# Moving small route steps to VectorE and the decode subtractions of attention to GpSimd

## The chip, the cores and the metric

The kernel runs on one core of a Trainium2 chip. The metric is the device time of one execution, in microseconds; the median of three runs is compared. The engines are named as in the profile: PE is TensorE's matmul side and PEld its weight loads, DVE is VectorE, ACT is ScalarE, POOL is GpSimd, SP is SyncE, which here only issues DMAs. Each engine runs its own instructions strictly in the order in which they were written.

## The reference

Three layers follow each other: local attention with a distance bias, a mixture of experts with one expert per token, and a mixing layer (two Fourier transforms and a wide two-matmul block). Only the first two matter here.

```python
# attention, per batch b and head h (B=2, H=8, S=768, D=64; 8 global keys, 96 local keys)
scores = q @ k.T / sqrt(D) - slope[h] * dist     # kept where key is global or local
a = exp(scores - max); a = a / (sum(a) + 1e-9)
x = a @ v                                        # heads side by side: (B, S, 512)

# routing, token by token: the expert may be the previous token's
fresh = argmax(x @ w_gate)
e = fresh if s == 0 or sigmoid(x @ w_local) < 0.5 else previous e
p = softmax(x @ w_gate)
out = p[e] * (relu(x @ w1[e]) @ w2[e])           # E=8 experts, 512 -> 1024 -> 512
```

## The kernel before

**Attention** (`fast_attention`). The 768 positions are cut into six tiles `i` = 0 to 5 of 128. A unit `n` is one tile, one batch entry `b` and one half `g` of the heads (four heads), so there are 24 units, four for each tile. The loop over `n` is a software pipeline written out by hand. In round `n` it writes, among others:

- `out(n - 2, 1)`: ACT copies the second half of a transposed probability tile out of PSUM (line 166);
- `keep(n - 3)`: DVE copies the product with v out of PSUM (line 179);
- `scores(n)`: PE (line 132), `rowmin(n)`: four DVE instructions that add the bias and find the row extreme `nm` (line 141);
- `transp(n - 1, 0)` and `transp(n - 1, 1)`: PE transposes (line 160), `expo(n)`: four exponentials on ACT (line 150) that also sum into `den`, and then the addition of 1e-9 to `den` (line 151);
- `upright(n - 3)`: PE (line 184), `norm(n - 3)`: DVE divides by `den` (lines 196, 199, 201);
- `values(n - 2)`: PE (line 174).

`patch_k` (line 104) and `patch_v` (line 109) put the eight global keys and values into the head of a tile that the next tile will read as its neighbour.

**Routing** (`Route.run`). After the fourth unit of a tile, a generator starts that finds the experts of its tokens. It is advanced between the steps of the later rounds, so a tile's route steps lie in the rounds of the next tile. It makes `lg` (line 481), the largest logits (507, 510), `gn` and `gf` (508, 514), `pe` (513), two PE transposes of `gn` and `gf` (517, 518), `rows` on ACT (521), the sum `su` (524, 528, 535), two scans over the tokens (532 `ex`, 541 `cu`), two small PE matmuls (546, 547), the rank `rk` (555), the probabilities into `xrow` (557) and the place `pos` of each token (565). Then SP writes the rows to `xs` (568) and POOL writes the token list by an indirect DMA (569). The engine `X` takes the steps 508, 513, 528 and 557: GpSimd, and VectorE for the last tile.

After tile 3 (`i == NT - 3` with NT = 6) SP reads the head of the list back (line 580) and POOL gathers the first tokens of expert 0 by an indirect DMA into `st.x0` (line 583), which `early` uses for expert 0's first matmuls.

**Decoding of expert pieces.** Four expert weight pieces are loaded during attention and split into a rounded high half and the rest: ACT casts (line 1007) and DVE subtracts (line 1009), in columns of 512. The table `TAKES` sets the rounds: group 0, 1, 2 and 3 with four columns each, 16 pairs in all. `Ring.take` uses DVE unless it is given another engine by `eng`.

**Behind attention** the list is read, tokens are gathered and the experts run (PE at work nearly throughout), then the mixing layer.

Of the kernel before, what the change touches and what calls it, by code (L numbers as in the profile page):

```python
# [18 lines left out]
ALU = mybir.AluOpType  # L19
# [8 lines left out]
NT = S // P  # L28
# [24 lines left out]
def load_kq(nc, st, io, i, pairs=((0, B * H // 2),)):  # L53

    if i >= NT:
        return
    for h, n in pairs:
        nc.sync.dma_start(st.kq[i][:, :, h:h + n], io["kq"][i, :, :, h:h + n])


def fast_attention(tc, st, io, route):
    nc = tc.nc
    V, A, G, T = nc.vector, nc.scalar, nc.gpsimd, nc.tensor
    KS = 3
    HP = B * H // 2
    with ExitStack() as ctx:
# [12 lines left out]
        four, last = views(st.raws, PIECES), views(more, NT - PIECES)  # L79
# [7 lines left out]
        def load_v(i):  # L87
            nc.sync.dma_start(vs[:, i % KS], io["v"][i])
# [45 lines left out]
        def rowmin(n):  # L134
            u = live[n]
            u.nm = wk.tile([P, 4], F32, name="nm")
            u.t = wk.tile([P, 4, 256], F32, name="t", bufs=3)
            for k in range(2):
                for j in range(2):
                    x = 2 * k + j  # L140
                    V.tensor_tensor_reduce(  # L141
                        out=u.t[:, x, :u.W], in0=u.sp[:, j, k, :u.W], in1=bias[:, 4 * u.g + x, u.b0:u.b0 + u.W],
                        scale=-0.125, scalar=3.0e38, op0=ALU.add, op1=ALU.min,
                        accum_out=u.nm[:, x:x + 1])

        def expo(n):
            u = live[n]
            u.den = wk.tile([P, 4, 1], F32, name="den", bufs=4)
            for x in range(4):
                A.activation(u.t[:, x, :u.W], u.t[:, x, :u.W], AF.Exp, bias=u.nm[:, x:x + 1], scale=-1.0, accum_out=u.den[:, x])  # L150
            G.tensor_scalar(u.den, u.den, 1e-9, None, op0=ALU.add)

        def transp(n, k):
            u = live[n]
# [7 lines left out]
        def out(n, k):  # L162
            u = live[n]
            if k == 0:
                u.p = wk.tile([P, 4, 2, P], F32, name="p")
            A.copy(u.p[:, 2 * k:2 * k + 2, :u.nk], u.tp[k][:, :, :u.nk])  # L166
# [9 lines left out]
        def keep(n):  # L176
            u = live[n]
            u.o = wk.tile([P, 2, P], F32, name="o")
            V.tensor_copy(u.o, turned)
# [44 lines left out]
        def far():  # L224
            d = local(prev, 0)
            V.tensor_tensor(d, d, gl, op=ALU.max)
            load_v(1)
            yield
            yield from tables(0, 256)
            load_kq(nc, st, io, 2)  # L230
            load_kq(nc, st, io, 3)
# [10 lines left out]
        bg = Background()  # L242
        bg.add(near)
        units = [(i, b, g) for i in range(NT) for b in range(B) for g in range(2)]
# [12 lines left out]
        def step(k):  # L257

            for at, g, lo, hi in TAKES:
                if k == at:  # L260
                    bg.add(st.ring.take("e", g, cols=512, follow=False, part=(lo / 4, hi / 4)))
            route.slot = k % 4
            bg.step()
            for _ in range(AHEAD.get(k, 0)):
                next(ahead, None)

        for n in range(N + 3):
            if ok(n):
                i, b, g = units[n]
                first = (b, g) == (0, 0)  # L270
                if (b, g) == (1, 0) and 0 < i < NT - 1:
                    load_v(i + 1)
                if first and i > 0:
                    load_kq(nc, st, io, i + 3)
                if i >= 2 and (b, g) == ((1, 0) if i < NT - 1 else (0, 0)):

                    st.ring.load(i - 2)
            if n == 1:
                bg.add(far())
            k = 4 * (n - N)  # L280
            if ok(n - 2):
                out(n - 2, 1)
            if ok(n - 3):
                keep(n - 3)
            if ok(n):
                scores(n)
                rowmin(n)
                if units[n][2]:
                    patch_k(*units[n][:2])
            if ok(n - 3) and not ok(n - 1):  # L290
                upright(n - 3)
                norm(n - 3)
            step(k)
            if n < len(BUSY):
                keep_busy(nc, st, ps_t.tile([P, 2, 2, P], F32, name="tp").rearrange("p a b n -> p (a b n)"), BUSY[n])
            if ok(n - 1):
                transp(n - 1, 0)
            if ok(n):
                expo(n)
            if ok(n - 1):  # L300
                out(n - 1, 0)
            step(k + 1)
            if ok(n - 1):
                transp(n - 1, 1)
                if ok(n - 3):
                    upright(n - 3)
                    norm(n - 3)
            step(k + 2)
            if ok(n - 2):
                values(n - 2)  # L310
                if units[n - 2][2]:
                    patch_v(*units[n - 2][:2])
            step(k + 3)
            if n == 2:
                G.tensor_copy(gk, st.kq[0][:, 0, :, :GMAX])
            if ok(n - 3):
                live.pop(n - 3)
# [10 lines left out]
def general_attention(tc, st, io, route):  # L328
# [3 lines left out]
    with ExitStack() as ctx:  # L332
# [18 lines left out]
        for i in range(NT):  # L351
# [11 lines left out]
            for b in range(B):  # L363
                x = rt.tile([P, ROW], F32, name="xrow")
                xs.append(x)
                for h in range(H):
# [16 lines left out]
                    V.tensor_tensor(t, t, far, op=ALU.add)  # L383
                    V.tensor_reduce(out=m, in_=t, op=ALU.max, axis=AX.X)
                    V.tensor_scalar(m, m, -1.0, None, op0=ALU.mult)
                    A.activation(t, t, AF.Exp, bias=m)
                    V.tensor_reduce(out=m, in_=t, op=ALU.add, axis=AX.X)
                    V.tensor_scalar(m, m, 1e-9, None, op0=ALU.add)
# [40 lines left out]
class Route:  # L429
# [31 lines left out]
    def run(self, i, xs, parts=None):  # L461
        nc, st, sb = self.tc.nc, self.st, self.sb
        V, A, G, T = nc.vector, nc.scalar, nc.gpsimd, nc.tensor
# [9 lines left out]
        pp = sm[:, 0:B]  # L473
        other = sm[:16, 4:5]
        last, soon = i == NT - 1, i in (NT - 3, NT - 2)
        X = V if last else G
        to = lambda s, n=1: self.at(None if last else s, n)
        from2, from1 = st.pairs[:16, 0:16], st.pairs[:16, 16:32]
        lg = sb.tile([P, B, NL], F32, name="lg")
        if parts is not None:  # L480
            V.tensor_reduce(out=lg.unsqueeze(3), in_=parts.rearrange("p b h e -> p b e h"), op=ALU.add, axis=AX.X)
        else:
# [23 lines left out]
        for b in range(B):  # L506
            V.max(m8[:, b], l8[:, b])
        X.tensor_scalar(gn, z.to_broadcast([P, B, E]), GATE, None, op0=ALU.is_ge)
        for b in range(B):
            V.max_index(ix[:, b], m8[:, b], l8[:, b])  # L510
        yield from to(3 if soon else 1)
        V.tensor_copy(fr, ix[:, :, :1])
        X.tensor_tensor(pe, l8, m8[:, :, :1].to_broadcast([P, B, E]), op=ALU.subtract)
        V.scalar_tensor_tensor(gf, z.to_broadcast([P, B, E]), GATE, fr.to_broadcast([P, B, E]),
                               op0=ALU.is_lt, op1=ALU.mult)
# [7 lines left out]
        yield from to(1)  # L523
        V.tensor_reduce(out=su, in_=pe, op=ALU.add, axis=AX.X)
        if last:
# [3 lines left out]
        if last:  # L529
# [3 lines left out]
                             op0=ALU.mult, op1=ALU.add)  # L533
# [8 lines left out]
                             op0=ALU.mult, op1=ALU.add)  # L542
# [1282 lines left out]
```

## Time and profile before

| | |
|---|---|
| median of three runs | 658.94 us (657.78 to 660.36) |
| the profiled execution | 660.04 us |
| its span in the trace | 658.3 us |
| granted TensorE clock, mean | 0.983 |
| busy: PE / PEld / DVE / ACT / POOL | 95% / 77% / 60% / 42% / 13% |

The span is the time from the first to the last instruction of the trace; the 1.7 us beside it are around the program. The chain of waits that the profile follows back from the end begins only at about 308 us, so it says nothing of attention, which takes the first 115 us; attention is read from the timelines of the engines. In a timeline a row gives the start, the duration, the engine, the line and the operation, and in brackets the idle time ahead of it with what ended it. Starts of neighbouring rows can lie closer than a duration, since instructions of one engine overlap at their ends.

### The profile page before, as it was taken

To read this page: it belongs to the slowest core of one execution; us is meant where nothing else is said; L and a number is where in the kernel's file an instruction comes from. 1 tells how busy PE (TensorE), PEld (TensorE's weight loads), DVE (VectorE), ACT (ScalarE), POOL (GpSimd) and SP (SyncE) were. 2 spreads that over 40 slices of the span, in tenths; PEclk is the share of its full clock that TensorE was granted. 3 is DMA by queue.
4 is the path that set the end of the run, shared out by engine and by line. 5 is a ranking of instruction groups with operands and counts; after the bars stand their busy time and mean duration, and the time that the engine had idled before them with its cause. 6 is when DMAs were issued, how large, how long until landed. Compare 5 with 4: busy or idle time off the path is not lost.

```text
span 658.3 us, 9969 instructions
## 1 busy us (share of the span) xinstructions
PE 622.8 (95%) x3621; PEld 509.3 (77%) x3622; DVE 392.3 (60%) x906; ACT 279.3 (42%) x562; POOL 83.0 (13%) x133
## 2 busy tenths in 40 slices
PE   7999985869999999999999899999999999999997
PEld 3777754659988998897867687877788888888886
DVE  4789885418958688844368977899451141254112
ACT  5888783218455666654433533542221121141110
POOL 1133222230431332320100000000000000000000
PEclk9999997869999999999999999999999999999999
DMA  8354460557898798884053133453010010100001
GB/s 295 150 195 135 131 99 20 133 167 259 327 367 297 255 319 296 311 335 142 10 206 140 65 127 129 134 185 129 0 65 0 1 65 1 65 0 1 0 1 64
DMA packets 25219, 92.49 MB, mean 140 GB/s; under 512 B 7660, under 2 KB 8812, under 8 KB 17216
## 3 DMA queue, kind: packets, MB, share of 16 engines
q1 hardware_dynamic: 19408, 77.44, 34.7%
q0 software_dynamic: 4736, 10.56, 4.4%
q10 hardware_dynamic: 1008, 3.65, 1.5%
q8 instruction: 35, 0.57, 0.4%
q14 instruction: 32, 0.26, 0.2%
HBM read 81.03 MB, written 14.84 MB: 146 GB/s over the span
## 4 chain that ended last, share of the span: by engine, by line
PE 39%; DVE 11%; ACT 2%; issue 1%; DMA 1%; DVEq 0%; ACTq 0%
PE h L1637 17%; PE acc L1653 5%; PE acc L1652 5%; PE acc L1651 5%; DVE dec L1033 1%; DVE dec L1035 1%; PE y L1142 1%; PE more L1192 1%; PE more L1142 1%; PE h L1192 1%; DVE dec L1031 1%; DVE dec L1029 1%; DMA u<-x 1%; PE f L1603 1%; DVE wide L987 1%
## 5 line engine op out<-in xcount | busy, mean ns | idle before, releaser
L1642 DVE SCALAR_TENSOR_TENSOR hl<-h,hh 128x512 fp32r<-128x512 f32 x48 | 33.0, 688 | 118.0 <-ACT hh L1641 118.0
L1641 ACT ACTIVATE hh<-h 128x512 fp32r<-128x512 f32 x48 | 28.6, 596 | 153.2 <-PE h L1637 153.2
L1009 DVE TENSOR_TENSOR wide<-raws,wide 128x1024 fp32r<-128x1024 f32 (+2 forms) x46 | 50.5, 1111 | 25.8 <-ACT wide L1007 25.7
L150 ACT ACTIVATE t<-t,nm 128x256 f32<-128x256 f32 (+1 forms) x96 | 45.8, 478 | 9.5 <-DVE nm L141 9.5
L1007 ACT CAST wide<-raws 128x1024 fp32r<-128x1024 f32 (+2 forms) x46 | 43.3, 957 | 5.3 <-PE acc L1653 3.4
L1637 PE MATMUL h<-un0h,wide 128*128 128x512 f32 (+1 forms) x136 | 42.5, 378 | 0.1
L1652 PE MATMUL acc<-wide,hh 128*128 128x512 f32 x96 | 37.8, 394 | 0.0
L1653 PE MATMUL acc<-wide,hl 128*128 128x512 f32 x96 | 37.6, 391 | 0.0
L1651 PE MATMUL acc<-wide,hh 128*128 128x512 f32 x96 | 37.5, 391 | 0.0
L141 DVE CUSTOM_DVE_ANT_0 t<-sp,bias 128x256 f32<-128x256 f32 (+1 forms) x96 | 32.7, 395 | 6.7 <-ACT p L166 2.9
L1165 ACT ACTIVATE hh<-h 128x512 fp32r<-128x512 f32 x28 | 16.7, 598 | 31.7 <-PE h L1162 29.4
L1072 POOL DMA_INDIRECT xg<-xs,ent x23 | 27.5, 1196 | 15.7 <-issue 6.1
L160 PE MATMUL tp<-consts,t 128*128 128x128 f32 x176 | 27.2, 290 | 2.4 <-ACT p L166 1.9
L1637 PEld LDWEIGHTS h<-un0h,wide 128*128 128x128 f32 x136 | 25.0, 188 | 5.0 <-ACT un0h L1413 0.3
L1162 PE MATMUL h<-xh,wide 128*128 128x256 f32 x192 | 28.4, 284 | 0.2
L160 PEld LDWEIGHTS tp<-consts,t 128*128 128x128 f32 x176 | 19.6, 144 | 11.0 <-ACT p L166 6.6
L1162 PEld LDWEIGHTS h<-xh,wide 128*128 128x128 f32 x192 | 25.5, 192 | 1.0 <-ACT sl5h L1007 0.5
L1166 DVE SCALAR_TENSOR_TENSOR hl<-h,hh 128x512 fp32r<-128x512 f32 x28 | 19.2, 685 | 11.8 <-ACT hh L1165 9.6
L1637 PE MATMUL h<-un0l,wide 128*128 128x512 f32 (+1 forms) x68 | 25.6, 377 | 0.0
L174 PE MATMUL sm<-p,vs 128*64 128x128 f32 x352 | 24.5, 279 | 0.0
L166 ACT COPY p<-tp 128x512 f32<-128x512 f32 (+1 forms) x48 | 24.2, 533 | 0.0
L1035 DVE SCALAR_TENSOR_TENSOR dec<-raws,dec 128x1024 int32<-128x1024 int32 x18 | 22.0, 1225 | 0.6
(450 smaller groups left out, 1635.5 us busy)
## 6 DMA issues: line engine op xcount, KB each, us to landing
raws<-we SPq DMA_DIRECT2D x30, 1024.0 KB
raws<-wm SPq DMA_DIRECT2D x17, 1024.0 KB
raws<-wmf SPq DMA_DIRECT2D x7, 1024.0 KB
wmf<-dec POOLq DMA_DIRECT2D x8, 512.0 KB, 9.0
xs<-xrow SPq DMA_DIRECT2D x12, 260.0 KB
vs<-v SPq DMA_DIRECT2D x6, 512.0 KB
raws<-kq SPq DMA_DIRECT2D x3, 1024.0 KB
u<-x SPq DMA_DIRECT2D x6, 512.0 KB
```

Of the source, the lines that this page charges most:

```text
L141: V.tensor_tensor_reduce(out=u.t[:, x, :u.W], in0=u.sp[:, j, k, :u.W], in1=bias[:, 4 * u.g + x, u.b0:u.b0 + u.W], scale=-0.125, scalar=3.0 ...
L150: A.activation(u.t[:, x, :u.W], u.t[:, x, :u.W], AF.Exp, bias=u.nm[:, x:x + 1], scale=-1.0, accum_out=u.den[:, x])
L160: T.transpose(u.tp[k][:, j, c], u.t[:, 2 * k + j, c * P:(c + 1) * P], st.ident)
L1007: (first or nc.scalar.copy)(hi[:, cs], raw[:, cs])
L1009: (eng() if callable(eng) else eng or nc.vector).tensor_tensor(lo[:, cs], raw[:, cs], hi[:, cs].bitcast(F32), op=ALU.subtract)
L1162: T.matmul(ps[:, u], w[:, f], x[:, k], start=n == 0, stop=n == 11)
L1637: nc.tensor.matmul(ps[:, c], a[:, k], x[:, k, c], start=n == 0, stop=n == 11)
L1641: nc.scalar.activation(hh, ps, AF.Relu)
L1642: nc.vector.scalar_tensor_tensor(hl, ps, 0.0, hh.bitcast(F32), op0=ALU.max, op1=ALU.subtract)
L1651: T.matmul(acc[c], hh[:, cs], h2, start=first, stop=False)
L1652: T.matmul(acc[c], hh[:, cs], l2, start=False, stop=False)
L1653: T.matmul(acc[c], hl[:, cs], h2, start=False, stop=last)
```

## The change

There are four edits, all within attention and its routing:

1. the addition to `den` (line 151) is made by VectorE for the units of the last tile, and by GpSimd for the others as before;
2. the subtraction of the decode pairs in attention (line 1009) is given to GpSimd;
3. `patch_k` and `patch_v` are left out for the last tile, which has no next tile;
4. `X` is VectorE for the last two tiles (4 and 5) and not for the last one alone.

```diff
-            G.tensor_scalar(u.den, u.den, 1e-9, None, op0=ALU.add)
+            (G if u.i < NT - 1 else V).tensor_scalar(u.den, u.den, 1e-9, None, op0=ALU.add)
...
             for at, g, lo, hi in TAKES:
                 if k == at:
-                    bg.add(st.ring.take("e", g, cols=512, follow=False, part=(lo / 4, hi / 4)))
+                    bg.add(st.ring.take("e", g, cols=512, follow=False, part=(lo / 4, hi / 4), eng=lambda: G))
...
                 scores(n)
                 rowmin(n)
-                if units[n][2]:
+                if units[n][2] and units[n][0] < NT - 1:
                     patch_k(*units[n][:2])
...
                 values(n - 2)
-                if units[n - 2][2]:
+                if units[n - 2][2] and units[n - 2][0] < NT - 1:
                     patch_v(*units[n - 2][:2])
...
         last, soon = i == NT - 1, i in (NT - 3, NT - 2)
-        X = V if last else G
+        X = V if i >= NT - 2 else G
```

The first place is on POOL at the end of attention. `list<-dest,pos` is the list write of a tile, `vs<-xs,ent_89` the gather of expert 0's first tokens, `gn`, `pe`, `su` and `xrow` are the route steps of tile 4, `wide` is a low half of an expert piece. Before:

```order
L569 DMA list<-dest,pos 12416x2 x2
L151 TENSOR_SCALAR den<-den 128x4
L583 DMA vs<-xs,ent_89 128x520
L508 TENSOR_SCALAR gn<-lg 128x16
L513 TENSOR_TENSOR pe<-lg,m_1489 128x16
L104 COPY kq<-gk 128x4x8
L151 TENSOR_SCALAR den<-den 128x4
L528 TENSOR_SCALAR su<-su 128x2
L557 TENSOR_SCALAR xrow<-pe,su 128x8 x2
L569 DMA list<-dest,pos 12416x2 x4
```

And after:

```order
L557 TENSOR_SCALAR xrow<-pe,su 128x8 x2
L1009 TENSOR_TENSOR wide<-raws,wide 128x512 x2
L569 DMA list<-dest,pos 12416x2 x2
L1009 TENSOR_TENSOR wide<-raws,wide 128x512 x2
L583 DMA vs<-xs,ent_89 128x520
L1009 TENSOR_TENSOR wide<-raws,wide 128x512 x4
L569 DMA list<-dest,pos 12416x2 x4
```

Behind the gather there stand now four subtractions and the list writes, and no route step of tile 4.

The second place is on DVE, the stretch in which tile 4's gates are made; `lg` are its logits, `o` is `keep`'s copy. Before:

```order
L1009 TENSOR_TENSOR wide<-raws,wide 128x512
L196 RECIPROCAL rs<-den 128x4
L199 TENSOR_TENSOR lgp<-mi,rs 128x40
L201 TENSOR_TENSOR xrow<-mi,rs 128x256
L481 TENSOR_REDUCE lg<-lgp 128x20
L507 MAX m_1489<-lg 128x8 x2
L510 MAX_INDEX ix<-m_1489,lg 128x8 x2
L512 CAST fr<-ix 128x2
L514 SCALAR_TENSOR_TENSOR gf<-lg,fr 128x16
L1009 TENSOR_TENSOR wide<-raws,wide 128x512
L179 COPY o<-sm 128x256
```

And after:

```order
L151 TENSOR_SCALAR den<-den 128x4
L196 RECIPROCAL rs<-den 128x4
L199 TENSOR_TENSOR lgp<-mi,rs 128x40
L201 TENSOR_TENSOR xrow<-mi,rs 128x256
L481 TENSOR_REDUCE lg<-lgp 128x20
L507 MAX m_1488<-lg 128x8 x2
L508 TENSOR_SCALAR gn<-lg 128x16
L510 MAX_INDEX ix<-m_1488,lg 128x8 x2
L512 CAST fr<-ix 128x2
L513 TENSOR_TENSOR pe<-lg,m_1488 128x16
L514 SCALAR_TENSOR_TENSOR gf<-lg,fr 128x16
L179 COPY o<-sm 128x256
```

Two subtractions are gone from there, `gn` and `pe` have come in, and at the head stands the addition to `den`, which reads what the exponentials of the same round sum up.

## Rows read from the trace of the kernel before

**Rows 1.** The page: busy time, share of the span and instructions of each engine.

```profile
PE 622.8 (95%) x3621; PEld 509.3 (77%) x3622; DVE 392.3 (60%) x906; ACT 279.3 (42%) x562; POOL 83.0 (13%) x133
```

**Rows 2.** Stretches: length, each engine's busy time (instructions), granted clock, DMA share, GB/s.

```profile
97.00:104.20 7.20, 0.26 (x3) 0.06 (x2) 3.56 (x19) 1.21 (x3) 1.62 (x4) 0.73 0.01 1
...
180.00:260.00 80.00, 79.36 (x503) 71.03 (x504) 62.40 (x79) 47.51 (x61) 21.10 (x21) 1.00 0.84 298
```

**Rows 3.** Timeline of POOL around 103 us: start, duration, operation, idle time and releaser.

```profile
102.67 1.11 POOL L583 DMA_INDIRECT vs<-xs,ent  x1 [5.54 <-DMA ent<-list]
103.81 0.28 POOL L508 TENSOR_SCALAR gn<-lg 128x16 bf16<-128x16 f32 x1
```

**Rows 4.** Timeline of SP's queue: the read of the list's head.

```profile
99.63 0.33 SPq L580 DMA_DIRECT2D ent<-list  x1
```

**Rows 5.** Timeline of PE in attention.

```profile
56.19 1.14 PE L132 MATMUL sp<-raws 64*128 64x256 f32 x8
...
58.21 0.66 PE L160 MATMUL tp<-consts,t 128*128 128x128 f32 x4 [0.29 <-ACT p L166]
...
60.64 1.13 PE L132 MATMUL sp<-raws 64*128 64x256 f32 x8
...
64.48 0.49 PE L132 MATMUL sp<-raws,kq 64*128 64x128 f32 x4
...
79.50 0.22 PE L517 MATMUL sm<-identb,gn 128*16 128x128 bf16 x1 [1.38 <-DVE o L179]
...
87.03 0.20 PE L546 MATMUL sm<-cu,consts 16*16 16x1 f32 x2
...
104.14 0.28 PE L517 MATMUL sm<-identb,gn 128*16 128x128 bf16 x1 [6.94 <-POOL gn L508]
```

**Rows 6.** Timeline of ACT: exponentials and their sums.

```profile
54.61 0.51 ACT L150 ACTIVATE t<-t,nm 128x256 f32<-128x256 f32 x1 [0.42 <-DVE nm L141]
...
87.51 0.19 ACT L150 ACTIVATION_READ_ACCUMULATOR t<-t,nm 128x1 f32 x1
...
94.67 0.51 ACT L150 ACTIVATE t<-t,nm 128x256 f32<-128x256 f32 x1 [0.43 <-DVE nm L141]
...
105.46 0.50 ACT L150 ACTIVATE t<-t,nm 128x256 f32<-128x256 f32 x1
```

**Rows 7.** Timeline of DVE in attention.

```profile
53.21 0.69 DVE L1009 TENSOR_TENSOR sl0l<-raws,sl0h 128x512 fp32r<-128x512 f32 x1
...
88.71 0.75 DVE L1009 TENSOR_TENSOR wide<-raws,wide 128x512 fp32r<-128x512 f32 x1 [0.75 <-ACT wide L1007]
...
96.19 0.17 DVE L196 RECIPROCAL rs<-den 128x4 f32<-128x4 f32 x1
...
98.17 0.18 DVE L514 SCALAR_TENSOR_TENSOR gf<-lg,fr 128x16 bf16<-128x16 f32 x1
...
108.25 0.17 DVE L535 RECIPROCAL su<-su 128x2 f32<-128x2 f32 x1 [0.37 <-POOL su L528]
...
109.50 0.46 DVE L541 TENSOR_TENSOR_SCAN cu<-consts,cu,oh 16x128 f32<-16x128 f32 x1
...
111.91 0.41 DVE L179 COPY o<-sm 128x256 f32<-128x256 f32 x1
```

**Rows 8.** Waits of ACT from 46 to 135 us: total, times, longest.

```profile
ACT t L150 <- DVE nm L141: 5.2, 9, 0.9
```

**Rows 9.** Timeline of POOL: a full-width copy, two small copies, the last list write.

```profile
6.56 0.64 POOL L454 COPY iw<-consts 128x512 f32<-128x512 f32 x1
...
69.78 0.51 POOL L104 COPY kq<-gk 128x32 f32<-128x32 f32 x1 [0.58 <-PE sp L132]
...
88.71 0.20 POOL L104 COPY kq<-gk 128x32 f32<-128x32 f32 x1
...
123.98 0.97 POOL L569 DMA_INDIRECT list<-dest,pos  x1 [6.80 <-DVE cnt L604]
```

**Rows 10.** Timeline of DVE behind attention: the two probability products on VectorE.

```profile
122.33 0.35 DVE L557 TENSOR_SCALAR xrow<-pe,su 128x8 f32<-128x8 f32 x2
```

## The prediction

> **What bounds the kernel now.** I read the page first, then a table of stretches, then the timelines of the four compute engines through attention, since the change touches nothing behind it. By the page PE is busy 95% of the span [rows 1], so the question is where PE is not busy within attention, and whether time won there reaches the end. In the experts it does: from 180 to 260 us PE works 79.36 of 80 us [rows 2], the weights are loaded as that work frees their buffers, and the first gathers wait for the token list that attention leaves. So I count a microsecond won in attention as a microsecond at the end.
>
> Within attention one hole stands out. From 97.0 to 104.2 us PE works 0.26 us of 7.2, and the granted clock of that stretch is 0.73, between the two levels of 1.2 and 2.4 GHz [rows 2]. The timelines say why. POOL stands at the gather of expert 0's first tokens, which waits for the list's head, issued on SP at 99.63; the gather starts at 102.67 after 5.54 us of idling, and only behind it comes `gn` of tile 4, at 103.81 [rows 3, 4]. PE's transposition of `gn` at 104.14 has waited 6.94 us for it [rows 5], and in PE's queue stand all the transposes of the last units. `gn` itself needs only the logits, which DVE has by 97.4. It is a wait in a queue, not for data.
>
> The rest of attention is nearer to its bounds. PE starts the scores of a unit at 60.64 and of the next at 64.48 [rows 5], 3.84 us with no wait. The unit ahead, 56.19 to 60.64, took 4.45: 0.13 of route matmuls more, and 0.48 lost where a transpose had to wait until 58.21 for ACT's copy. ACT was that late because it had itself stood 0.42 us at 54.61 for `nm` from DVE [rows 6], and DVE had just spent 0.69 on a subtraction at 53.21 [rows 7].
>
> **The change part by part.** All times are on the clock of the profiled execution.
>
> *The 16 subtractions leave DVE.* That is 16 of about 0.69 us [rows 7], 11 us of DVE time; but DVE is not the bound. ACT's waits for `nm` are 5.2 us in all [rows 8], which is the most ACT can win, and PE wins less, because it is at its own pace of 3.84 us whenever ACT is on time. Up to 80 us PE has three holes that hang on DVE: 0.48 in group 0, the same 0.47 in group 1, and the 1.38 at 79.50, where the transposition of tile 3's gates waits for `gf` and `keep`'s copy at the end of a DVE queue that has just made two subtractions [rows 5]. The lower bound of this part is 0.95 (the third hole stays), the upper 2.3 (all close). Without its two subtractions the DVE queue ahead of 79.50 is 1.2 us shorter, so I take **2.0**. Below nothing I see only by way of the port, a rival below.
>
> *On POOL* a subtraction of 128x512 does not occur in this trace. The nearest row is a copy of 128x512, 0.64 us [rows 9]; two inputs may double it, 1.28, and I take 1.2. Pairs come every 4.4 us in the decode rounds, so POOL, 13% busy [rows 1], holds them easily. The Trainium skill (GPSIMD Engine Reference, "Performance versus the Vector engine") calls GpSimd the wrong choice for ordinary elementwise work and gives 4497 ns for such an operation of 2048 columns; an estimate from that page is a quarter, 1.12 us, and the sum would be the same by it. Behind the subtractions stand the list writes. Those of tile 3 come after two subtractions whose casts are done by 89.7, so they are through by about 92, when `pos` is made; the gather and the reading of the list's head are not held. The last four run behind the gather, to about 109, and the list of tile 4 is only wanted at about 110.
>
> *Tile 4's route steps go to DVE.* This removes the wait of 6.94. What is late next is DVE's own chain, because the third addition to `den` of tile 5 now stands at its head and waits for the exponentials of its round: they start at 94.67 in the trace [rows 6], at 94.5 with DVE relieved, and four of 0.49 and the reading of the sum end at 96.55; `den` is done at 96.7. From `rs` at 96.19 to the end of `gf` at 98.35 [rows 7] is 2.16 us, plus `gn` and `pe`, 0.35 for both at the 0.18 of their neighbour: `gf` at 99.2, `keep`'s copy at 99.6, PE at **99.66 instead of 104.14: 4.5 us**. ACT's last exponentials then start at 101.0 instead of 105.46 [rows 6].
>
> Some of it is given back. The last `den` waits for these exponentials to 103.0, and ten DVE instructions now stand behind it which in the trace went ahead: `cu` comes at 105.4 instead of 109.50 [rows 7], 4.1 won. In the trace `su` had its own wait for POOL there, at 108.25, and it goes. Then two products of `xrow`, 0.35 by the same pair on VectorE at 122.33 [rows 10], stand ahead of `keep`'s copy at 111.91 [rows 7]: 3.8 won. From there on the queues are the same as before. So this part is **3.8**, at most 4.5 (nothing given back), at least 2.5 if PE's clock falls all the same in the 2 us in which it still stands still.
>
> *The additions to `den` on DVE* cost 0.15 each, but the wait counts: the first of them stands ahead of `cu` of tile 3, and PE's small matmul on `cu`, at 87.03 [rows 5], has all of PE's work behind it. The sums are read to 87.70 [rows 6], so it starts at about 88.45 and PE loses 1.4 us. Its cover is ACT: the next exponentials start at 90.17 in the trace, and with DVE's subtraction gone `nm` is there at 90.2 in spite of the wait. PE runs a unit behind ACT and takes the loss out of what it had ahead, so I cost it at nothing; without the cover it is 1.4.
>
> *The patches of the last tile* are two copies of 0.2 us on POOL and two small DMAs on SP. Nobody reads them; SP's rows of tile 4 no longer queue behind a patch, but are wanted much later. Nothing.
>
> Sum: 2.0 + 3.8 = 5.8 us. The profiled execution took 660.04, so 654.2 by its own time; it is 1.1 above the median of the runs, 658.94, and the changed kernel's median comes to **653.1**.
>
> **The rivals.**
>
> *The two engines get in each other's way.* A POOL copy of 128x32 takes 0.20 at 88.71 but 0.51 at 69.78 [rows 9], where a DVE subtraction was under way; at 88.71 both started together, and there DVE's took 0.75 instead of 0.69 [rows 7]. So the one that comes second waits. Now POOL's are the long ones, and DVE's scan `cu` and rank `rk`, each with two inputs, could wait for them: `rk` of tile 3, some 0.85, and behind the gather, where four subtractions follow each other without a gap, `cu` and `rk` of tile 4, 0.6 and 1.2. That is 2.7 of the 5.8: 655.8. For it: the row at 69.78. Against it: most of DVE's work here reads one input from PSUM, and other POOL rows beside such work are not lengthened. The Trainium skill (SBUF — State Buffer, "Who interferes with whom") has this as a rule, an exclusive lock for an operation of DVE with two SBUF inputs against a GpSimd one that reads SBUF, held by whichever starts first; by it this rival would be the forecast. The rows at 69.78 and 88.71 agree with it; how often the two meet, no row tells.
>
> *The additions to `den` cost what I put at nothing*, and the holes before 80 us stay at half: 5.8 less 1.4, less 1.0, less a further 1.0 for the tail: 656.5. For it: DVE now waits for ACT four times while ACT waits for DVE in each round, a ring with little slack. Against it: the working above, unit by unit.
>
> *Better than forecast:* nothing is given back in the tail, and the full 2.3 before it with a further 1 of the 5.2 us of ACT's waits: 651.1.
>
> *Slower: POOL becomes the bound.* Four subtractions and the list write of tile 4 stand between the gather, done at 104.3, and the last tile's list write, wanted at 120.2 (123.98 [rows 9] less 3.8); the list takes 2.7. That is room for four of 3.3 us. From 4.75 us each the whole gain is gone, and at 6 us each the time is 663.9. For it: the operation has no row here. Against it: the copy of the same width at 0.64.
>
> *The change doesn't do what it says* would be that PE's transposition finds another wait on POOL; but tile 4 then has nothing on POOL ahead of its list write, so this has no chance of its own.
>
> **How the numbers follow.** Forecast 0.53, at 651.9 to 654.5; the port 0.20; `den` 0.12; better 0.09; slower 0.06. The range runs from 650.2, a microsecond under the better case for what a median of three moves, to 657.4, a microsecond over the worst of the cases that gain; outside are the slower case and the ends. Half a per cent, 3.3 us, is about what a measurement of this kernel can tell from no change, so faster means below 655.6: the forecast, the better case and a third of the port case, 0.69. Within: the rest of the port and `den`, 0.25. Slower 0.06.
>
> **What would show it.** In the changed kernel's trace PE's wait ahead of the transposition of tile 4's `gn` must be 1 to 3 us, and end with DVE and not with POOL; the waits of ACT for `nm` must fall below 3 us in total; POOL's subtractions must last 1.0 to 1.5 us; and the expert stage must begin 5 to 6 us earlier, with the same length. I am wrong if scans and ranks on DVE last 1 us or more beside POOL's subtractions (the port), if PE's wait for `cu` in tile 5's first rounds shows up in ACT's exponentials (`den`), or if the list writes wait for POOL itself.

## The result, and the profile after

| | before | after |
|---|---|---|
| median | 658.94 us | 664.09 us (663.01 to 665.37) |
| ratio after to before, 95% interval | | 1.0081 (1.0060 to 1.0101) |
| the profiled execution | 660.04 us | 663.01 us |
| its span | 658.3 us | 661.2 us |
| granted clock, mean | 0.983 | 0.981 |

The change makes the kernel slower by 0.8%. The forecast was 653.1, and its range ended at 657.4. The two profiled executions lie 2.9 us of span apart, the medians 5.2: the profile after is of the fastest of its five runs, and the other four had a mean granted clock of 0.975 to 0.977. No trace tells where these ran slower still, so what follows explains the 2.9 by rows and the rest by other kernels' medians.

The page after, against [rows 1]: PE has the same work and a point less of the span; POOL has the subtractions.

```profile
PE 623.5 (94%) x3621; PEld 511.5 (77%) x3622; DVE 391.2 (59%) x899; ACT 279.2 (42%) x562; POOL 98.5 (15%) x138
```

The table of stretches, columns as in [rows 2]:

```profile
97.00:104.20 7.20, 4.01 (x28) 3.60 (x30) 4.94 (x25) 3.65 (x14) 3.15 (x4) 0.76 0.12 26
104.00:112.00 8.00, 3.98 (x36) 3.23 (x34) 6.55 (x14) 2.50 (x6) 3.74 (x4) 0.90 0.05 21
112.00:122.00 10.00, 6.98 (x44) 5.21 (x42) 5.35 (x29) 1.06 (x3) 2.00 (x2) 0.67 0.46 160
...
180.00:260.00 80.00, 79.40 (x510) 71.50 (x510) 62.89 (x79) 46.91 (x60) 22.43 (x22) 1.00 0.84 297
```

The two middle stretches before:

```profile
104.00:112.00 8.00, 7.33 (x62) 5.95 (x62) 5.08 (x17) 5.90 (x17) 1.97 (x7) 0.81 0.14 39
112.00:122.00 10.00, 7.55 (x47) 5.59 (x47) 5.66 (x28) 1.06 (x3) 2.09 (x2) 0.83 0.62 114
```

The old hole is more than half filled: from 97.0 to 104.2 PE works 4.01 us instead of 0.26. But in the next 8 us it works 3.98 instead of 7.33. The clock, 0.81 in these 8 us before, behind the old hole, is 0.90 there now, and 0.67 in the 10 us that follow, behind a new one. (The 0.83 of before in those 10 us lies further on, where PE waits for tile 5's gates: in steps of 2 us the clock is 1.00 from 108 to 116 us and 0.50 from 118 to 120.) The experts' stretch is as full as before. PE's timeline after, against [rows 5], names the holes:

```profile
77.88 0.22 PE L517 MATMUL sm<-identb,gn 128*16 128x128 bf16 x1 [1.39 <-DVE o L179]
...
86.94 0.20 PE L547 MATMUL sm<-cu,consts 16*16 16x1 f32 x2 [1.10 <-DVE cu L541]
...
89.89 1.09 PE L174 MATMUL sm<-p,vs 128*64 128x128 f32 x16
...
100.19 0.27 PE L517 MATMUL sm<-identb,gn 128*16 128x128 bf16 x1 [3.84 <-DVE o L179]
...
109.75 0.77 PE L184 MATMUL mi<-iw,o 128*128 128x148 f32 x4 [4.02 <-DVE o L179]
110.45 1.98 PE L174 MATMUL sm<-p,vs 128*64 128x128 f32 x16
...
114.94 1.98 PE L174 MATMUL sm<-p,vs 128*64 128x128 f32 x16
...
119.89 0.22 PE L517 MATMUL sm<-identb,gn 128*16 128x128 bf16 x1 [1.04 <-DVE gn L508]
```

The row of before for the last of these, the transposition of tile 5's gates with which attention ends:

```profile
117.22 0.22 PE L517 MATMUL sm<-identb,gn 128*16 128x128 bf16 x1 [1.13 <-DVE gn L508]
```

So tile 3's gates come 1.62 us earlier than before (77.88 for 79.50), tile 4's 3.95 earlier (100.19 for 104.14), and tile 4's wait for DVE instead of POOL; yet tile 5's come 2.67 later, and the span ends 2.9 later. All that is lost goes between 100 and 120 us. The one wait of 6.94 us has become two, of 3.84 and 4.02, 7.86 together. Behind the second `values` takes 1.98 where it took 1.09 at 89.89, the lower of the two clock levels after PE had stood still.

What PE waits for there is `o`, `keep`'s copy, at the end of a queue on DVE. DVE's timeline after, with the rank `rk` of tile 3 and the third and fourth addition to `den`:

```profile
87.50 1.28 DVE L555 SCALAR_TENSOR_TENSOR rk<-cu,sm,oh 16x128 f16<-16x128 f32 x1
...
95.61 2.12 DVE L151 TENSOR_SCALAR den<-den 128x4 f32<-128x4 f32 x1 [1.11 <-ACT t L150]
...
98.96 0.15 DVE L508 TENSOR_SCALAR gn<-lg 128x16 bf16<-128x16 f32 x1
...
103.60 4.17 DVE L151 TENSOR_SCALAR den<-den 128x4 f32<-128x4 f32 x1 [2.09 <-ACT t L150]
```

POOL's timeline in the same place, in place of [rows 3]:

```profile
87.37 2.55 POOL L1009 TENSOR_TENSOR wide<-raws,wide 128x512 fp32r<-128x512 f32 x2 [3.32 <-ACT wide L1007]
...
95.19 2.49 POOL L1009 TENSOR_TENSOR wide<-raws,wide 128x512 fp32r<-128x512 f32 x2
101.71 1.05 POOL L583 DMA_INDIRECT vs<-xs,ent  x1 [4.02 <-PE tp L160]
102.79 4.95 POOL L1009 TENSOR_TENSOR wide<-raws,wide 128x512 fp32r<-128x512 f32 x4
```

An addition of 4 numbers in each lane takes 2.12 and 4.17 us, where `gn`, of the same kind and four times as large, takes 0.15. Each of the two ends with POOL's row of subtractions, to 0.05 us: 95.61 + 2.12 = 97.73 and 95.19 + 2.49 = 97.68; 103.60 + 4.17 = 107.77 and 102.79 + 4.95 = 107.74. And ahead of each stands an idle time for ACT, the longest 2.09. The waits of after from 46 to 135 us, against [rows 8] (total, times, longest), say the same:

```profile
PE mi L184 <- DVE o L179: 5.6, 3, 4.0
DVE den L151 <- ACT t L150: 5.4, 4, 2.1
...
ACT t L150 <- DVE nm L141: 3.4, 4, 1.2
```

ACT waits 1.8 us less for `nm` than before, but DVE now waits 5.4 for ACT, which is new.

### The profile page after: what moved, and what is told of

Same layout as the page of the kernel before. It is cut to its first block, busy times and chain, and to the rows that moved or that the text cites. A ratio compares the mean times of both kernels' runs of the same rounds, so it can differ in the third digit from the quotient of the medians.

```text
span 661.2 us, 9961 instructions
## 1 busy us (share of the span) xinstructions
PE 623.5 (94%) x3621; PEld 511.5 (77%) x3622; DVE 391.2 (59%) x899; ACT 279.2 (42%) x562; POOL 98.5 (15%) x138
## 4 chain that ended last, share of the span: by engine, by line
PE 38%; DVE 11%; ACT 2%; issue 1%; DMA 1%; DVEq 0%; ACTq 0%
PE h L1637 17%; PE acc L1653 5%; PE acc L1652 5%; PE acc L1651 5%; DVE dec L1033 1%; DVE dec L1035 1%; PE y L1142 1%; PE more L1192 1%; PE more L1142 1%; PE h L1192 1%; DVE dec L1031 1%; DVE dec L1029 1%; DMA u<-x 1%; PE f L1603 1%; DVE wide L987 1%
## 5 line engine op out<-in xcount | busy, mean ns | idle before, releaser
L1009 DVE TENSOR_TENSOR wide<-raws,wide 128x1024 fp32r<-128x1024 f32 (+1 forms) x38 | 45.0, 1200 | 24.3 <-ACT wide L1007 24.3
L174 PE MATMUL sm<-p,vs 128*64 128x128 f32 x352 | 26.4, 293 | 0.0
L174 PEld LDWEIGHTS sm<-p,vs 128*64 128x64 f32 x352 | 20.2, 145 | 3.9 <-issue 3.6
```

The costliest lines, as they stand in the source:

```text
L174: T.matmul(turned[j * D:j * D + D, k], vs[:, ti % KS, u.h + 2 * k + j], u.p[:, 2 * k + j, c], start=c == 0, stop=c == len(tiles) - 1)
L1009: (eng() if callable(eng) else eng or nc.vector).tensor_tensor(lo[:, cs], raw[:, cs], hi[:, cs].bitcast(F32), op=ALU.subtract)
```

## The experiments

The theory: the additions to `den` on DVE cost twice. Written behind the exponentials of the same round, they make DVE stand still until ACT is through (the place); and they meet POOL's subtractions and are held by them (the port). The rivals: the subtractions alone cost, whatever stands on DVE; or tile 4's route steps cost on DVE. Edits are numbered as in the section on the change. Each short diff, its lines shortened to what changes and `...` for lines left out, is against the changed kernel unless it says otherwise; ratios are to the kernel before, timed on the same chip. The runs lie on three chips, four on each in the order given, and there the kernel before took 658.6, 658.5 and 658.3 us, beside the 658.9 of the result. A difference of two medians from different chips is uncertain by these tenths besides the intervals, so below the same difference by the ratios stands beside it.

**No subtractions on POOL** (edits 1, 3 and 4).

```diff
-  take("e", g, cols=512, follow=False, part=(lo / 4, hi / 4), eng=lambda: G)
+  take("e", g, cols=512, follow=False, part=(lo / 4, hi / 4))
```

> The change without its second edit: the subtractions stay on VectorE. Port theory (the addition to den on VectorE cannot go on while GpSimd subtracts, 2.0 and 4.0 us in the last two rounds of tile 5): each addition lasts about 0.2 us, the transposition of tile 4's gates stands at about 100.7 us instead of 104.1, 0.7 of it is given back, and the time is 655.5 to 657.5. Order theory (what costs is that the addition waits for the exponentials with all of VectorE behind it, port or not): no faster than the kernel before, 659 to 664. POOL theory (GpSimd itself comes late with its lists because of the subtractions): 653 to 656, with GpSimd's list writes earlier than before.

Measured 657.9, ratio 0.9984 (0.9971 to 0.9998), between the range of the port theory and that of the order theory: by the runs below both have a part.

**`den` back on POOL** (edits 2, 3 and 4).

```diff
-  (G if u.i < NT - 1 else V).tensor_scalar(u.den, u.den, 1e-9, None, op0=ALU.add)
+  G.tensor_scalar(u.den, u.den, 1e-9, None, op0=ALU.add)
```

> The change without its first edit: the additions to den of tile 5 stay on GpSimd, the subtractions are there too. Port theory: no VectorE operation of one value per partition and scalar meets the long run of subtractions behind the gather, PE's 4.0 us wait for keep's copy is gone, 652 to 656; if the small scalar operations of tile 4's route fall into that run, one of them lasts several us in the addition's place and the time is 657 to 662. Order theory: 652 to 656 as well, but no operation of VectorE lengthened. POOL theory: 660 to 664, the list of the last tile late.

Measured 657.62, ratio 0.9988 (0.9972 to 1.0005). Undoing either edit takes away about 6 us of the loss, so neither explains it alone, and neither leaves more than 1.5 us of the forecast gain. Nor is `den` all that is held. DVE's timeline of this kernel:

```profile
94.36 1.78 DVE L508 TENSOR_SCALAR gn<-lg 128x16 bf16<-128x16 f32 x1
96.53 1.25 DVE L513 TENSOR_TENSOR pe<-lg,m 128x16 f32<-128x16 f32 x1
102.07 1.67 DVE L537 TENSOR_SCALAR oh<-ex,consts 16x128 f16<-16x128 f32 x1
104.00 1.58 DVE L541 TENSOR_TENSOR_SCAN cu<-consts,cu,oh 16x128 f32<-16x128 f32 x1
```

These are 0.15, 0.17, 0.25 and 0.46 in the kernel without subtractions on POOL. But the additions on POOL break up its rows of subtractions: `gn` and `oh` end at 96.14 and 103.74, where POOL's additions start (96.19 and 103.73 in its timeline).

**The same sum by a reduction.** ACT's sums of the last tile's units go into pairs with 1e-9 beside each, and DVE adds a pair by `tensor_reduce`.

```diff
+  pairs = res.tile([P, 4, 4, 2], F32, name="pairs")
+  G.memset(pairs, 1e-9)
...
+  part = pairs[:, n % 4] if u.i == NT - 1 else u.den
...
-  (G if u.i < NT - 1 else V).tensor_scalar(u.den, u.den, 1e-9, None, op0=ALU.add)
+  if u.i < NT - 1:
+      G.tensor_scalar(u.den, u.den, 1e-9, None, op0=ALU.add)
+  else:
+      V.tensor_reduce(out=u.den, in_=part, op=ALU.add, axis=AX.X)
```

> The whole change, but the addition to den of tile 5 is made on VectorE as a reduction over pairs (sum, 1e-9) instead of an addition of a scalar: same place in the order, same wait for ACT, subtractions on GpSimd. Port theory in its narrow form (only operations of one input with a scalar, and those with two inputs, wait for GpSimd): the reduction lasts 0.2 us in all four rounds, 653.5 to 656.5. Wide form (everything on VectorE from memory to memory waits): 2 and 4 us as in the change, 662 to 665. Order theory: 662 to 665, with the reduction at 0.2 us.

Measured 664.83, ratio 1.0084 (1.0061 to 1.0107): the time did not move, but the wait did. DVE's and then POOL's timeline of this kernel (its line numbers are 6 higher behind the edit):

```profile
96.85 0.16 DVE L157 TENSOR_REDUCE den<-pairs 128x4 f32<-128x8 f32 x1 [1.11 <-ACT t L153]
...
103.35 0.16 DVE L157 TENSOR_REDUCE den<-pairs 128x4 f32<-128x8 f32 x1 [1.99 <-ACT t L153]
...
103.62 5.09 DVE L534 TENSOR_SCALAR su<-su 128x2 f32<-128x2 f32 x1
```

```profile
96.42 2.50 POOL L1015 TENSOR_TENSOR wide<-raws,wide 128x512 fp32r<-128x512 f32 x2
102.67 1.05 POOL L589 DMA_INDIRECT vs<-xs,ent  x1 [3.75 <-PE sm L180]
103.75 4.93 POOL L1015 TENSOR_TENSOR wide<-raws,wide 128x512 fp32r<-128x512 f32 x4
```

The reduction at 96.85 runs in 0.16 in the midst of two subtractions, and PE's wait at tile 4's gates falls from 3.84 to 2.45. The reduction at 103.35 is through before POOL's row of four begins. The next scalar operation behind it, the `su` that edit 4 has moved there, then takes 5.09 us for two numbers in each lane and ends at 108.71, with POOL's row at 108.68. What is held is a kind of operation, and if one gets by, the next is held. The time alone and the short reduction are also what the order theory had expected; that holding has a part in it rests on `su` here, and on the runs below that change the row and the place one at a time. The Trainium skill (SBUF — State Buffer, "Who interferes with whom") states that on this chip a reduction never contends with GpSimd while a tensor_scalar can; the rows at 96.85 and 103.62 agree. It also has the loser blocked for the other's whole instruction; here the instruction is 1.28 us and the wait four of them, so by the measurement that is not the upper end.

**The same sum with two inputs from SBUF.**

```diff
-  (G if u.i < NT - 1 else V).tensor_scalar(u.den, u.den, 1e-9, None, op0=ALU.add)
+  if u.i < NT - 1:
+      G.tensor_scalar(u.den, u.den, 1e-9, None, op0=ALU.add)
+  else:
+      V.scalar_tensor_tensor(u.den, u.den, 1e-9, u.den, op0=ALU.add, op1=ALU.max)
```

> The whole change, but the addition to den of tile 5 is an operation with two inputs from memory (den + 1e-9, then the larger of that and den), which is the kind that waited 1.28 us in the change's rk. If such a one waits for one subtraction at most and not for the whole row of them: up to 1.3 us in each of the last two rounds, 655 to 659. If it waits as the scalar addition does: 2 and 4 us, 662 to 665. Order theory: 662 to 665 whatever it lasts.

Measured 664.36, ratio 1.0073 (1.0047 to 1.0098), and DVE's timeline has the same wait:

```profile
95.91 2.11 DVE L154 SCALAR_TENSOR_TENSOR den<-den 128x4 f32<-128x4 f32 x1 [1.11 <-ACT t L150]
...
103.85 4.29 DVE L154 SCALAR_TENSOR_TENSOR den<-den 128x4 f32<-128x4 f32 x1 [2.04 <-ACT t L150]
```

So neither form escapes, and for this kernel it does not matter which it is.

**The route steps and patches alone** (edits 3 and 4): both edits above undone.

> Only the third and fourth edit: tile 4's route steps on VectorE, the last tile's patches left out; the subtractions stay on VectorE and the additions to den on GpSimd. Port theory: nothing on GpSimd that reads memory for long, so no operation of VectorE is lengthened, PE's transposition of tile 4's gates is released by VectorE at about 100 us instead of 104.1, and the time is 654 to 656.5. Give-back theory (what is won ahead of the gather is lost again behind it, since the last tile's chain hangs on something else): 657.5 to 659.

Measured 654.54, ratio 0.9935 (0.9922 to 0.9949). The gain that the forecast gave to edit 4 is there. PE's timeline: the wait is 2.15 us, ended by DVE. The first row behind it is still at the upper clock level (0.22, as at 79.50 in [rows 5]), but the eight transposes that follow take 1.76, where eight take 1.09 a little later: the clock falls here too, for a shorter time.

```profile
99.02 0.22 PE L517 MATMUL sm<-identb,gn 128*16 128x128 bf16 x1 [2.15 <-DVE o L179]
...
99.23 1.76 PE L160 MATMUL tp<-consts,t 128*128 128x128 f32 x8
...
103.40 1.09 PE L160 MATMUL tp<-consts,t 128*128 128x128 f32 x8
```

This kernel and the one without subtractions on POOL differ by edit 1 alone, 654.5 to 657.9: **3.4 us (3.2 by the ratios) for the additions on DVE with no subtractions on POOL to hold them.** Each lasts 0.17 there. What it costs is read from ACT's first exponential of each of the last four rounds, here and then there:

```profile
85.34 0.51 ACT L150 ACTIVATE t<-t,nm 128x256 f32<-128x256 f32 x1 [0.82 <-DVE nm L141]
...
89.84 0.51 ACT L150 ACTIVATE t<-t,nm 128x256 f32<-128x256 f32 x1 [0.43 <-DVE nm L141]
...
94.33 0.51 ACT L150 ACTIVATE t<-t,nm 128x256 f32<-128x256 f32 x1 [0.43 <-DVE nm L141]
...
100.22 0.50 ACT L150 ACTIVATE t<-t,nm 128x256 f32<-128x256 f32 x1
```

```profile
86.50 0.51 ACT L150 ACTIVATE t<-t,nm 128x256 f32<-128x256 f32 x1 [0.82 <-DVE nm L141]
...
91.42 0.51 ACT L150 ACTIVATE t<-t,nm 128x256 f32<-128x256 f32 x1 [0.85 <-DVE nm L141]
...
96.62 0.51 ACT L150 ACTIVATE t<-t,nm 128x256 f32<-128x256 f32 x1 [1.14 <-DVE nm L141]
...
103.86 0.51 ACT L150 ACTIVATE t<-t,nm 128x256 f32<-128x256 f32 x1
```

The three steps are 4.50, 4.49 and 5.89 us with the additions on POOL, and 4.92, 5.20 and 7.24 with them on DVE: 0.42, 0.71 and 1.35 lost, 2.5 in all, and some more in the last round. That the second rows begin 1.16 later is not the edit's doing: that execution is 1.07 later already at ACT's exponentials near 21 us (22.05 for 20.98). It is a ring: the addition waits for ACT's exponentials, all that DVE does for the next `nm` stands behind the addition, and ACT's next exponentials wait for `nm`.

**Subtractions of groups 0 and 1 on POOL** (edits 3 and 4 beside it, `den` on POOL).

```diff
-  part=(lo / 4, hi / 4), eng=lambda: G)
+  part=(lo / 4, hi / 4), eng=(lambda: G) if g < 2 else None)
```

> As the run before, and the subtractions of groups 0 and 1 on GpSimd (those of 2 and 3 on VectorE). Port theory: in the rounds of groups 0 and 1 the subtractions come singly, VectorE's small operations wait at most 1.3 us there and PE's two holes of 0.5 us and half of the 1.4 us at 79.5 close: 1 to 2 us faster than the run before, 652.5 to 655. If the subtractions on GpSimd cost VectorE there what they save: equal to the run before.

Measured 654.01, ratio 0.9931 (0.9918 to 0.9944). PE reaches tile 3's gates at 78.31 instead of the 79.22 of edits 3 and 4 alone, tile 4's at 98.34 instead of 99.02, but in the medians the half microsecond is less than the intervals can tell. The two early groups are harmless, and nearly worthless.

**The subtractions alone** (edit 2, and nothing else of the change).

> Only the second edit: the subtractions on GpSimd, everything else as before. Port theory: the additions to den are on GpSimd's own queue, tile 4's steps too, so VectorE meets the long run of subtractions only with its two scans, oh and rk, 1.3 us or less each; PE's wait of 7 us for gn behind the gather stays: 656.5 to 660. POOL theory (GpSimd's queue is overloaded by the subtractions): 661 or more, with gn, su or the lists late on GpSimd.

Measured 659.04, ratio 1.0014 (0.9998 to 1.0030). PE is at tile 3's gates 1.5 us earlier than before, and then waits 1.1 us longer for `gn` behind the gather, which comes only 0.95 earlier (101.72, for 102.67 in [rows 3]):

```profile
103.21 0.28 PE L517 MATMUL sm<-identb,gn 128*16 128x128 bf16 x1 [8.05 <-POOL gn L508]
```

Part of what is won ahead of the gather is given back in the wait for it. Behind it `oh` takes 1.32 and `cu` 1.17 beside POOL's last three.

**The changed kernel with the last four subtractions back on DVE.**

```diff
-  part=(lo / 4, hi / 4), eng=lambda: G)
+  part=(lo / 4, hi / 4), eng=(lambda: G) if g < 3 else None)
```

> The whole change, but the four subtractions of group 3, which stand behind the gather, stay on VectorE; groups 0 to 2 are on GpSimd, the additions to den of tile 5 on VectorE. Port theory: the last addition to den falls from 4.2 to 0.2 us, the one ahead of it stays near 2.1 (two subtractions of group 2 in a row); PE's wait for keep's copy falls from 4.0 to 0.5 us and its half clock behind it goes: 657.5 to 660. Order theory: 662 to 665 as the change.

Measured 657.72, ratio 0.9984 (0.9975 to 0.9993): taking the row of four behind the gather away from POOL wins 6.4 us, as much as taking all sixteen away (6.2, from 664.1 to 657.9); by the ratios both are 6.4. The third addition is still held, 2.13 us; the fourth takes 0.17, after its wait of 2.09 for ACT. So the loss by holding in the change is made by the row of four; the other twelve cost nothing on balance there.

**The first three groups on POOL, `den` on POOL** (edits 3 and 4 beside it).

> The kernel with edits 3 and 4, the addition to den on GpSimd as in the kernel before, and the subtractions of groups 0, 1 and 2 on GpSimd; those of group 3 on VectorE. With no subtraction of the decode on GpSimd this took 654.5, with those of groups 0 and 1 654.0, with all four groups 657.6. Theory that the price of the subtractions comes from back-to-back rows beside scalar operations of VectorE: group 2 meets rk, and group 3 gn, oh, cu and xrow, so most of the price is group 3's: 654.5 to 655.3 here. Rival, that each pair costs about the same wherever it is: 656. Rival, that the price is the chance of the runs: no difference to 654.0 or 657.6 that can be named.

Measured 655.95, ratio 0.9967 (0.9953 to 0.9982). With `den` on POOL the price of the subtractions by groups is: none for groups 0 and 1, 1.9 for group 2 (654.0 to 656.0), and 1.7 for group 3 (to 657.6); by the ratios 2.4 and 1.4, and the intervals of the last two overlap, so how the price divides between groups 2 and 3 is not settled. I had put nearly all on group 3, wrongly; the rival's figure of 656 is right, though not for its reason, since the early groups cost nothing. Group 2 meets `gn` and `pe`, not `rk` as I had expected. DVE's timeline, then PE's:

```profile
95.65 1.79 DVE L508 TENSOR_SCALAR gn<-lg 128x16 bf16<-128x16 f32 x1
...
97.83 1.26 DVE L513 TENSOR_TENSOR pe<-lg,m 128x16 f32<-128x16 f32 x1
```

```profile
100.16 0.26 PE L517 MATMUL sm<-identb,gn 128*16 128x128 bf16 x1 [3.54 <-DVE o L179]
100.46 1.97 PE L160 MATMUL tp<-consts,t 128*128 128x128 f32 x8
```

PE waits 3.54 us instead of 2.15. Its next transposes run at the lower level, 1.97, as they also do with groups 0 and 1 alone (1.97 at 98.64); but `values` behind them take 1.98 here (103.34) and 1.15 there (101.53), so the clock is low for longer.

**The addition on DVE, but late.** Subtractions on DVE, edits 3 and 4; the last tile's addition is written three rounds later, right ahead of the reciprocal that reads it.

```diff
-  (G if u.i < NT - 1 else V).tensor_scalar(u.den, u.den, 1e-9, None, op0=ALU.add)
+  if u.i < NT - 1:
+      G.tensor_scalar(u.den, u.den, 1e-9, None, op0=ALU.add)
...
+  if u.i == NT - 1:
+      V.tensor_scalar(u.den, u.den, 1e-9, None, op0=ALU.add)
   V.reciprocal(rs, u.den)
```

> Edits 3 and 4, subtractions on VectorE, and the addition to den of the last tile's units on VectorE but written right ahead of the reciprocal that reads it, three rounds after the exponentials. With this addition on GpSimd the time was 654.5; with it on VectorE right behind the exponentials of its round 657.9. Theory that the place costs (VectorE stands still until ScalarE has read the sum, and all that is queued behind it is late): 654.3 to 655.3, and no wait for ScalarE ahead of the addition. Rival, that the operation or the larger load of VectorE costs: 657 to 658.

Measured 654.95, ratio 0.9947 (0.9930 to 0.9964). The operation on DVE costs nothing that can be told from 654.5; its place behind the exponentials cost 3.0 (657.9 to 654.95; 2.4 by the ratios, whose intervals do not meet). In DVE's timeline it has no wait:

```profile
101.63 0.15 DVE L198 TENSOR_SCALAR den<-den 128x4 f32<-128x4 f32 x1
```

**The late addition with groups 0 and 1 on POOL.**

> As the run with the late addition, and the subtractions of groups 0 and 1 on GpSimd. Theory that these two groups meet no scalar operation that matters: 653.5 to 655.0, so beside 654.0 with the addition on GpSimd. Rival (any subtraction on GpSimd costs once VectorE has the addition): 656 or more.

Measured 653.69, ratio 0.9939 (0.9917 to 0.9961), as with the addition on POOL.

**The whole change, with the late addition.**

> All of the changed kernel but for one thing: the addition to den of the last tile's units on VectorE stands right ahead of its reciprocal instead of behind the exponentials of its round. The changed kernel took 664.1; with the addition on GpSimd it took 657.6. Theory: the wait for ScalarE goes, and with it the part of the price that comes from standing still; but gn, su, cu, rk and now the addition still fall beside GpSimd's rows of subtractions and are held to their end: 657 to 660. Rival, that the place of the addition was all of the loss: 653 to 655. Rival, that being held by GpSimd was all of it: 662 to 664.

Measured 659.22, ratio 1.0012 (1.0000 to 1.0025). The place was 4.9 us of the changed kernel's loss (4.5 by the ratios). The other 4.3, from 654.95 with the same additions and the subtractions on DVE, is the port alone. In DVE's timeline the additions are short now, and `rk` is held in their stead; then PE's:

```profile
98.97 0.13 DVE L198 TENSOR_SCALAR den<-den 128x4 f32<-128x4 f32 x1
...
104.25 3.89 DVE L558 SCALAR_TENSOR_TENSOR rk<-cu,sm,oh 16x128 f16<-16x128 f32 x1 [0.67 <-PE sm L550]
```

```profile
97.06 0.22 PE L520 MATMUL sm<-identb,gn 128*16 128x128 bf16 x1 [1.56 <-DVE o L180]
...
108.80 1.36 PE L185 MATMUL mi<-iw,o 128*128 128x148 f32 x4 [4.59 <-DVE o L180]
```

Tile 4's gates come 3.1 us earlier than in the changed kernel, but the row of four makes a hole behind them, 4.59 us where it was 4.02, and again with PE at the lower level.

The medians with edits 3 and 4 in them, in us, with the ratio to the kernel before:

| subtractions on | `den` on POOL | `den` on DVE, late | `den` on DVE, in its round |
|---|---|---|---|
| DVE | 654.5 (0.9935) | 654.95 (0.9947) | 657.9 (0.9984) |
| POOL, groups 0 and 1 | 654.0 (0.9931) | 653.7 (0.9939) | |
| POOL, all | 657.6 (0.9988) | 659.2 (1.0012) | 664.1 (1.0081, the change) |

Along the upper row the place costs 3.0; down the columns the port costs 3.1, 4.3 and 6.2. By the ratios these are 2.4, and 3.5, 4.3 and 6.4. The last is more than the others, and in the trace after it is the addition itself, a link of the ring, that is held (103.60). That this is why the two prices add to more than their sum is argued; no run takes it apart.

## Why the prediction was wrong

*The additions to `den`, "costed at nothing": the step that failed.* Their place costs 2.4 to 3.4 us, by the run and the measure taken, with no subtraction on POOL at all. The working followed the first of the four up to PE's small matmul and took ACT as cover: the next exponentials at 90.17, `nm` at 90.2 in spite of the wait. PE's wait for `cu`, forecast at 1.4 without cover, was 1.10 (86.94), and the cover held to within 0.4 us for one round, which is what the first step of the ring lost (4.92 for 4.50). It was then not carried on to the next three rounds, where the loss grows to 0.71 and 1.35, because ACT's lateness is DVE's wait in the next. The cover was the other half of the same ring. I had the ring as a rival, at 0.12, and at 656.5 with other losses in it; without the subtractions the time was 657.9.

*The port, a rival at 0.20 and 2.7 us, and at nothing in the sum: the second step that failed, and the larger.* It was there in full and was mis-sized twice. It holds more kinds than the scans and ranks I had named: small scalar operations of DVE (`den`, `su`, `gn`, `oh`) too, 0.15 to 0.25 us long when free. And the wait is not one subtraction but can be a whole row of them, up to 5.09 us. So the price is 3.1 with `den` on POOL, 4.3 with it late and 6.2 in the change. The bound I had drawn, the rest of a single subtraction for `rk` and `cu`, was no bound.

*The clock.* The forecast kept 2.5 instead of the 3.8 for the case that the clock falls all the same. With edits 3 and 4 alone it fell behind a wait of 2.15 us, and they gained 4.0 nevertheless. In the change the loss has grown: behind the hole at 109.75 two `values` took 0.89 more each than at the upper level. What the granted clock lacks of full speed adds up from 104 to 122 us to 0.19 x 8 + 0.17 x 10 = 3.2 us before, and to 0.10 x 8 + 0.33 x 10 = 4.1 after; from 122 to 126 it is 1.00 before and 0.74 after, a further 0.26 x 4 = 1.0. These sums are upper bounds, since PE also stands still in parts of these stretches; from 97 to 104, where the clock was 0.73 and 0.76, PE worked 0.26 us before and 4.01 after, so the low clock cost next to nothing there before and something after.

*Tile 4's route steps, 3.8:* right. With edit 3, whose patches were not tried by themselves, they gave 4.0 (0.9935), and in the changed kernel PE's wait for tile 4's gates was ended by DVE as forecast. That it ended at 100.19, near the 99.66 of the forecast, is luck: the exponentials of that round started at 93.50 instead of 94.5, and the addition behind them was held for 2.12 us. The wait was 3.84, outside the 1 to 3 us that the forecast had named as a sign.

*The subtractions leaving DVE, 2.0:* right in the place and wrong in the worth. Up to tile 3's gates 1.6 us were won, though the hole of 1.39 at 77.88, most of which the 2.0 had counted in, did not close; ACT's waits for `nm` fell to 3.4 and not below 3. But by the medians groups 0 and 1 are worth 0.5 with `den` on POOL and 1.3 with it late (0.3 and 0.5 by the ratios), neither clear of the intervals, and edit 2 alone is worth nothing.

*On POOL, 1.2 us each:* measured 1.26 to 1.33. *POOL as the bound,* the slower case: no; the list write of tile 4 waits 9.80 us for `pos` at 117.54. The time went up by another way, and the slower case had 0.06 because I had tied it to POOL's own lateness alone.

Taken from the runs, the terms are: −4.0 for edits 3 and 4, +3.4 for edit 1, +6.2 for edit 2 on top of both, together +5.6. That this is near the measured +5.2 is no check: the terms are steps on one way from the kernel before to the changed one, so they must add up to it, but for what the chips differ. By another way, as the table shows, the shares are others.

## What to carry to other kernels

An instruction that waits for another engine is priced by what stands behind it in its queue, over all rounds: if the engine it waits for needs that queue for its next step, there is no cover, and the cure is to write the instruction where its input is long there (654.95 instead of 657.9). Work moved from VectorE to GpSimd is not gone from VectorE: look for every small scalar or two-input operation of VectorE beside it, take the whole row of GpSimd instructions as the length of its wait until a trace shows less, and keep such rows away from stretches in which VectorE is on the path. Edits 3 and 4 with the first two groups on GpSimd, and `den` on GpSimd or late, are the fastest versions measured: 0.9931 (0.9918 to 0.9944) and 0.9939 (0.9917 to 0.9961); edits 3 and 4 alone, at 0.9935, cannot be told from them.

## What the runs showed of the hardware that I had not expected

- A scalar or two-input operation of VectorE on 128x2 or 128x4 numbers, 0.17 us when free, lasted 2.11 to 5.09 us beside a row of two or four GpSimd subtractions of 1.28 us each, and ended with the row; a reduction of 128x8 lasted 0.16 in the midst of one.
- Within a row VectorE sometimes came in after a single subtraction: in the changed kernel `rk` of tile 3 ended at 88.78, soon after the first of the two that began at 87.37. What decides between one and the whole row no run here tells. An instruction of another kind on GpSimd between two subtractions (its `den`, 0.22 us) let it in the three times shown here (`gn` and `oh` with `den` on POOL, `gn` with three groups).
- With `den` on POOL, `gn` had already begun to wait at 94.36, 0.47 us ahead of the subtraction at 94.83, while GpSimd was at an indirect DMA write; `su` at 103.62, with the reduction, began 0.13 ahead of its row. Whether that write holds such an operation too was not tried.
